# An S4 mixer with a spatial-shift MLP on one core: paired PSUM banks, other parameter and spectrum layouts, a power on GpSimd, and a new order

## The chip, the core and the metric

The kernel runs on one core of one Trainium2 chip. The metric is the device time of one execution in microseconds; the time before is the median of three runs, 515.06 us (515.02 to 515.52). The engines are named as in the profile: PE multiplies matrices (PEld loads its weights beside it), DVE is VectorE, ACT is ScalarE, POOL is GpSimd, SP is SyncE, which here only issues DMAs. Each engine works through its own list of instructions in order.

## The reference, cut to what matters

One sequence of L = 2048 tokens with D = 512 channels, N = 128 states per channel, hidden width F = 1376.

```python
xn = layernorm(u)                                    # over the 512 channels
# A: state-space convolution
K  = einsum("dn,dnl,dn->dl", Cc, exp(dt*A * l), dt*Bc).real     # 512 x 2048, complex inside
y  = irfft(rfft(pad(xn.T)) * rfft(pad(K)))[:L].T + xn * Dskip
# B: spatial shift and MLP, on the same xn
h  = gelu(layernorm(xn) @ w1)                        # 512 -> 512
g  = quarters of h shifted by +1, -1, +2, -2 tokens
x1 = xn + g @ w2
x2 = x1 + gelu(layernorm(x1) @ w3) @ w4              # 512 -> 1376 -> 512
out = u + y * silu(x2)
```

## The kernel before

**Tiling.** X holds the whole sequence in SBUF as 16 tiles of 128 tokens by 512 channels, four bytes an element. Token-side steps take two tiles at a time. The Fourier transforms are matrix products in two stages with DRAM in between: `u_stage1` makes the first stage of the spectrum of xn and stores it to `scr_Ud`; the tables of the convolution kernel end in `scr_Kf`; `products` reads both back, does the second stage, multiplies and does the first inverse stage into `scr_Zd`; `inverse` reads that back and does the last stage.

**Stages.** (1) `loads` and `params`: X, w1 and the parameters come in; six 512 x 128 parameter arrays are read with channel r*128+p in partition p (`raw`, tiles rawA and rawC), DVE and ACT compute on them (tiles tm, pn), PE transposes the result, and ACT copies it into `par`. (2) `token_mixing`: `ln_first` (statistics on DVE, `rstd` as a Sqrt on ACT and a reciprocal on DVE), `x_pair` (transposed tokens), `h_pair` (w1, gelu), `u_stage1`, the scales of w3 and w4 and their split into two halves of 16 bits, `hs_pair` (w2 over shifted tiles, added to X), `ln_second`. (3) 16 chunks of 32 channels in `tables`: sines, cosines and exponentials on ACT, about ten wide products on DVE (tile wv), then matmuls wv into pc and kev into pc and pd. (4) `mlp`, eight groups of 256 tokens, each six steps of w3 (pb), gelu, w4 (pa). (5) `products`, 8 steps for each half of the channels: spectrum of K (kin, into pd in the first half, pc in the second), copy to kh, spectrum of xn (uin, into pd), four DVE operations for the complex product (tiles pr, kh), inverse (pr, into pc and pd), copies to z1e. (6) `gate` (silu on ACT), `inverse` (zin; product into X) and `finish` (X + residual, store).

**PSUM.** Eight banks of 512 columns are eight tiles: pa, pb, pc and pd with two each. A bank is read by an instruction of its own: an evacuation of two banks is two instructions.

**Order.** Nothing is scheduled on the chip. The operations are recorded in program order with their dependencies (`Plan.add`; a PSUM bank counts as one cell for each 32 partitions). ORDER is a written-out list of operation numbers: the engines' instructions are issued in that order, so it fixes each engine's list and what stands behind what. The suffix a or v says which of ACT and DVE takes an operation that both could do (`Either`). All instructions show as L312, the line that issues them, so they are told apart by tiles. Before the first data arrive, 40 dummy matmuls (ident into pa, `WARM`) run on PE.

**Lines that the prediction touches.** `rstd` 576, `loads` 601, `params` 626, `sums` 750 (its end copies pc and pd to k1e), `products` 812, `inverse` 875, `ln_first` 986, `u_stage1` 1053, `hs_pair` 1086, `ln_second` 1104, `mlp` 1130.

Of the kernel before, what the change touches and what calls it, by code (L numbers as in the profile page):

```python
# [110 lines left out]
8 31 0 7 88 3 4 78 89 90 91 22 21 103 105 106 104 92 107 108 2 109 6 93 94 95 5 79 110 111 96a 100a 80 81 82 83 14 112  # L111
113v 84 85 86 17 115v 44 16 42 114a 87a 15 41 43 97a 20 101 98 36 45 46 18 37 118a 72 102a 47 99v 116 48 50 9 51 121
10 122 49 52 23 143 117a 123 53 124 125 54 119 24 164 170 166 171 140 168 25 73a 141 167 165 126 169 551 127 55 172
128 59 173 120a 60 56 11 146 174 175 142 129 19 38 151a 176 27 61 177 57 130 178 39 179v 152a 180v 26 182v 183v 33
148a 144 40 181v 184 186a 131 62 229 28 187 145 147a 192 161 204v 185a 231 154 158 290 188a 132 134 288 70 205 553 150
149 230 292 156 227 153 195 197a 196v 200a 286 375 232 225 287 291 289 71a 293 228 226 294 543 233 295 162 234 544 296
133 235 201a 207a 189 208 373 297 298 199 136v 545 34 299 236 237 190 216 198 63 191 137 217a 193 210 374 202 300 138v
218a 211 304v 203 221v 65 194 64 546 238 371 13 222a 66 68 206 256 135 220 239 219 376 212 139 554 213 67 242v 223
240v 224 257a 258a 262a 261a 209 69 74 555 243v 30 75a 214 215 241v 259 260 277 244v 302v 250 251 278a 58 76 279a 253
252 247v 263 157 264 283a 254 268v 282a 379 245 246 317 248 249 372 163 271 548 549 159 160 265a 547 280 269 550 77a  # L120
# [12 lines left out]
503 518 749 670 495 750 751 686 774 775 516a 671a 672 761 418 701 702 673 755a 756 762a 767a 522a 768 769 770a 763 523
703 519a 687 688 517 524 771a 757 758 776 788 764 765 781 690 772 689 773 782 704 705 674a 675a 777a 520 691 789 692
778 783 525a 779 420 707 784a 785 723 795 802 724 803 693a 694 422 725 676a 706 796 677a 695 708 790a 791 729 678 726
727 728 797 709 526 804 730 780 816a 786 710 787 792 798a 799 805a 806 845 817a 818 696a 697a 794 698a 699a 793 820a
711 712 846 809 731 700 824 825 826 732 810 811 853 847 800 801 812a 713 714 715a 880 854 807 808 813 814 831 815 832
855 716 821a 856 857 849 923 717 718a 838 719a 499 848 819 850 851 822 827a 833 852 823 733 734 858 859 735 736 737a
828 829 830 496 1215 839 860 861 834a 488 720a 721a 477 862 901 902 1222 1223 863 1216 1217 491 840a 474 835 903 738
739 722 740a 741a 836 837 864 867 1224 865 1229 742a 743a 744 1218a 841 866 1236a 842 1225a 882 904 1230 1231 843 1244  # L140
868 869 870 1219 871 906 844 1220 1221 907 872a 944 945 905 873 874 910 875a 876a 1251 946 1226 877a 878a 883 881
1237a 1232a 1227 885a 908 1238 884a 947 948 886 1233 1228 949 1239 887 891 925 1252 888 1245 909 889 890 892 1240a
1241a 893 1246 1234 1235 894 1242 895 898a 912 1258 1247a 879 911 950 953 896a 913 899a 1259 500 1253 1243 897a 914
1265 1254a 1255 915a 900 924 916 917 918a 497 492 489 1266 919a 920a 1248 1249 475 987 478 988 921a 926 968 922 1267
# [1143 lines left out]
```

## Time and profile before

| | |
|---|---|
| median of three runs | 515.06 us |
| the profiled execution, its own time | 514.98 us |
| its span, first to last instruction | 513.1 us |
| busy share of the span: PE, PEld, DVE, ACT, POOL | 96%, 62%, 90%, 79%, 0% |
| ACT_TABLE_LOAD (ACT changes its set of functions) | 54, 69.3 us |
| DMA packets | 156433, of which 98321 under 512 B; 90.07 MB |
| HBM traffic over the span | 160 GB/s |

The span leaves out 1.9 us of the profiled execution's time. A group of instructions is shown as what it writes and reads, shapes, count, then busy time, the mean length of one in ns, and the engine's idle time just before. Lengths overlap where instructions are pipelined: busy time divided by the count is the pitch, and is the better price of one. In tables by stretch the columns are, for each engine, busy us and (instructions), then the granted PE clock, the DMA engines' busy share and GB/s.

### The profile page before, as it was taken

The page shows a single profiled execution, that of the slowest core. Times are in us where ns is not written, and L with a number is a line of the kernel's source. Part 1 is how long each engine was busy: PE and PEld are TensorE (multiplying, and loading weights), DVE is VectorE, ACT ScalarE, POOL GpSimd, SP SyncE. Part 2 cuts the span into 40 slices and gives each one's busy share as a digit, 9 for nine tenths or more (in the row PEclk, how much of TensorE's full clock was granted, in tenths as well). Part 3 has the DMA queues.
Part 4 walks back from the last instruction along what each step waited for, and adds up shares of the span by engine and source line. Part 5 has one row for each costly group of instructions (what it writes and reads, how often), then busy time and mean ns, then how long its engine had stood idle before and what let it go on. Part 6 is the DMA issues. An engine that isn't in the chain of part 4 may idle for free.

```text
span 513.1 us, 14564 instructions
## 1 busy us (share of the span) xinstructions
PE 491.4 (96%) x6209; PEld 315.6 (62%) x6209; DVE 461.7 (90%) x744; ACT 403.4 (79%) x675; POOL 0.7 (0%) x6
## 2 busy tenths in 40 slices
PE   8789999999999999999999999999999999999993
PEld 8656674674446776676566566755665656666541
DVE  4999999999999999999999999999976698777376
ACT  3999999979989899999979999997763652555240
POOL 0000000000000000000000000000000000000000
PEclk9899999999999999999999999999999999999998
DMA  8969997764628613715375556366499997987997
GB/s 215 248 168 260 284 253 242 167 144 125 165 50 170 108 37 42 105 29 76 105 151 119 147 126 123 105 125 187 98 218 220 276 319 213 302 264 223 300 314 201
DMA packets 156433, 90.07 MB, mean 176 GB/s; under 512 B 98321, under 2 KB 147729, under 8 KB 155985
## 3 DMA queue, kind: packets, MB, share of 16 engines
q1 hardware_dynamic: 151840, 84.68, 66.6%
q10 hardware_dynamic: 4528, 4.46, 3.1%
q8 instruction: 49, 0.80, 0.6%
q14 instruction: 16, 0.12, 0.1%
HBM read 52.95 MB, written 29.36 MB: 160 GB/s over the span
## 4 chain that ended last, share of the span: by engine, by line
PE 54%; DVE 35%; ACT 5%; issue 3%; DMA 1%; SPq 0%; DVEq 0%; ACTq 0%
PE pb L312 23%; PE pa L312 16%; DVE wv L312 13%; PE pc L312 10%; PE pd L312 5%; DVE X L312 5%; DVE stats L312 2%; DVE pr L312 2%; DVE ghl L312 2%; DVE eg L312 1%; ACT L312 1%; DVE tm L312 1%; ACT wv L312 1%; DVE kh L312 1%; DMA X<-in_A_u_dram 1%
## 5 line engine op out<-in xcount | busy, mean ns | idle before, releaser
L312 PE MATMUL pb<-x1T,w3h 128*128 128x256 f16 (+1 forms) x1056 | 124.2, 273 | 1.4 <-issue 1.1
L312 PE MATMUL pa<-w4h,ghl 128*128 128x512 f16 (+1 forms) x528 | 122.6, 380 | 0.0
L312 PEld LDWEIGHTS <-w3h 128*128 128x128 f16 (+1 forms) x1056 | 102.0, 100 | 27.3 <-issue 13.1
L312 PEld LDWEIGHTS <-ghl 128*128 128x128 f16 (+1 forms) x528 | 48.9, 98 | 61.5 <-issue 9.0
L312 ACT ACT_TABLE_LOAD x54 | 69.3, 1283 | 3.5 <-issue 2.0
L312 ACT ACTIVATE wv<-wv 128x2080 f32<-128x2080 int32 x32 | 62.8, 1967 | 1.6 <-DVE wv L312 1.5
L312 DVE SCALAR_TENSOR_TENSOR ghl<-g,wsc,ghl 128x512 f16<-128x512 f32 (+1 forms) x48 | 33.3, 698 | 6.6 <-ACT ghl L312 6.5
L312 ACT ACTIVATE g<-pb,wsc 128x512 f32<-128x512 f32 (+1 forms) x48 | 30.5, 652 | 9.7 <-PE pb L312 5.4
L312 DVE TENSOR_TENSOR wv<-wv,eg 128x2048 f32<-128x2048 f32 x16 | 36.5, 2284 | 1.2 <-ACT wv L312 1.1
L312 DVE TENSOR_TENSOR wv<-mag,wv 128x2048 f32<-128x2048 f32 x16 | 36.5, 2283 | 0.0
L312 ACT ACTIVATE ghl<-g,wsc 128x512 f16<-128x512 f32 (+1 forms) x37 | 26.1, 707 | 10.7 <-PE pa L312 8.0
L312 PEld LDWEIGHTS pc<-wv 128*32 128x32 f32 x2048 | 29.8, 109 | 6.6 <-issue 2.4
L312 ACT ACTIVATE mag<-par 128x128 f32<-128x128 f32 x132 | 32.8, 459 | 0.9 <-DVE wv L312 0.9
L312 PE MATMUL pc<-wv 128*32 128x64 f32 x2048 | 32.4, 220 | 0.7 <-DVE wv L312 0.6
L312 ACT ACTIVATE wv<-wv,halfpi 128x2080 f32<-128x2080 f32 x16 | 32.9, 2056 | 0.2
L312 PE MATMUL pb<-xT,w1h 128*128 128x256 f16 x240 | 27.7, 273 | 0.0
L312 DVE TENSOR_TENSOR pr<-pd,kh 128x512 f32<-128x512 f32 x32 | 20.6, 685 | 7.6 <-PE pd L312 7.2
L312 PE MATMUL pa<-w,hT 128*128 128x512 f32 x58 | 26.3, 597 | 0.8 <-ACT ue L312 0.8
L312 PEld LDWEIGHTS <-w1h 128*128 128x128 f16 x240 | 22.8, 98 | 6.0 <-issue 2.6
L312 PE MATMUL pb<-w,hT 128*128 128x512 f32 x58 | 26.4, 596 | 0.0
L312 DVE BATCH_NORM_STATS2 stats<-X 128x6 f32<-128x512 f32 x32 | 21.3, 679 | 5.5 <-DMA X<-in_A_u_dram 5.5
L312 ACT COPY z1e<-pc 128x256 f32<-128x256 f32 x24 | 8.7, 381 | 21.6 <-PE pd L312 21.6
(158 smaller groups left out, 848.1 us busy)
## 6 DMA issues: line engine op xcount, KB each, us to landing
wst<-in_B_w_dram SPq DMA_DIRECT2D x20, 512.0 KB, 4.8
scr_Ud<-ue SPq DMA_DIRECT2D x32, 256.0 KB, 3.0
uin<-scr_Ud SPq DMA_DIRECT2D x16, 512.0 KB, 4.8
scr_Kfa<-k1e SPq DMA_DIRECT2D x8, 512.0 KB, 5.0
cst<-c_gp SPq DMA_DIRECT2D x16, 256.0 KB, 5.2
kin<-scr_Kfa SPq DMA_DIRECT2D x8, 512.0 KB, 4.4
scr_Kfb<-k1e SPq DMA_DIRECT2D x8, 512.0 KB, 6.6
scr_Zda<-z1e SPq DMA_DIRECT2D x8, 512.0 KB, 3.6
```

What stands on the lines that cost most here:

```text
L312: ins = [getattr(self.engines[op.eng], name)(*args, **kw).ins for name, args, kw in op.calls]
```

## The change

- **Paired banks.** Each pair of PSUM banks is also one tensor of 1024 columns (`two`). Where both banks of a pair were read one after the other, one instruction reads both: the copies ue, kh, k1e and z1e, the complex product, the additions in `hs_pair` and `mlp`, the product in `inverse`.
- **Parameters.** Partition p now holds channels 4p to 4p+3, so each row of an array is 2 KB in one piece where it was four pieces of 512 B; log_dt comes as 128 pieces of four numbers where it was 512 single ones. The copy into `par` puts the channels back in order.
- **Spectra.** `scr_Ud` keeps all 512 channels of a token together: one store for each tile (16 of 512 KB) where there were two (32 of 256 KB). The reads take half of each row.
- **Reciprocal roots.** In `ln_first` from tile 4 on and in `ln_second`, Sqrt on ACT and reciprocal on DVE become two instructions on POOL: add EPS, then raise to -0.5.
- **Order.** ORDER is new throughout.

By engine the program has: PE the same matmuls; DVE 746 instructions, now 630; ACT 682, now 588, with 54 and 47 ACT_TABLE_LOAD; SP 226, now 210; POOL 11, now 23.

DVE at the start. rawC holds B and C, tm products of them, stats the norm's statistics, X the tokens. Before:

```order
L312 BN_STATS stats<-X 128x6
L312 MEMSET epst 128x1
L312 MEMSET ones 1x128
L312 MEMSET ssq 128x16
L312 BN_AGGR mv<-stats 128x2
L312 TENSOR_SCALAR rs<-mv 128x1
L312 RECIPROCAL rs<-rs 128x1
```

And now:

```order
L311 TENSOR_TENSOR tm<-rawC 128x512 x3
L311 TENSOR_TENSOR tm<-tm 128x512
L311 TENSOR_TENSOR tm<-rawC 128x512
L311 BN_STATS stats<-X 128x6
L311 BN_AGGR mv<-stats 128x2
L311 TENSOR_SCALAR rs<-mv 128x1
L311 RECIPROCAL rs<-rs 128x1
```

Five products on the parameters, which stood behind the first four tiles' statistics, now stand ahead of the first. On SP, whose list began with four loads of X, the four of rawC now come first (two halves of X still go out on ACT's queue at once):

```order
L311 DMA rawC<-in_A_C_re_dram 128x512
L311 DMA rawC<-in_A_B_re_dram 128x512
L311 DMA rawC<-in_A_C_im_dram 128x512
L311 DMA rawC<-in_A_B_im_dram 128x512
L311 DMA X<-in_A_u_dram 64x512 x2
L311 DMA X<-in_A_u_dram 64x1024 x2
```

ACT in the first norm, tiles 8 to 15 (rs is the reciprocal root, ue the evacuated first stage, hT the gelu). Before:

```order
L312 ACTIVATE x2h<-X,rs 128x512
L312 ACT_TABLE_LOAD
L312 ACTIVATE rs<-mv,epst 128x8 x2
L312 ACT_TABLE_LOAD
L312 ACTIVATE hT<-pb_94 128x512
L312 COPY ue<-pa_91 128x512
L312 ACTIVATE wst,ssq<-wst 128x1024
L312 COPY ue<-pa_92 128x512
```

And now, about the same place:

```order
L311 ACTIVATE hT<-pb 128x512
L311 ACTIVATE wst,ssq<-wst 128x1024
L311 COPY ue<-pd 128x1024
L311 COPY ue<-pa 128x1024
L311 ACT_TABLE_LOAD
L311 ACTIVATE mag<-par 128x128 x11
```

The two roots and the pair of table loads around them are gone, and a copy takes two banks.

DVE at the end, from the last addition of the MLP (X<-pa) on. Before, its first rows:

```order
L312 SCALAR_TENSOR_TENSOR X<-pa_91,wsc,X 128x512
L312 SCALAR_TENSOR_TENSOR X<-pa_92,wsc,X 128x512
L312 TENSOR_TENSOR X<-X,pd_98 128x256
L312 TENSOR_TENSOR X<-X,pd_97 128x256
L312 TENSOR_TENSOR X<-X,pc_96 128x256
L312 TENSOR_TENSOR X<-X,pc_95 128x256
L312 TENSOR_TENSOR X<-X,pd_97 128x256
L312 TENSOR_TENSOR X<-X,xr 128x4x256
```

And now:

```order
L311 SCALAR_TENSOR_TENSOR X<-pa,wsc,X 128x1024
L311 TENSOR_TENSOR X<-X,pd 128x2x256
L311 TENSOR_TENSOR X<-X,pc 128x2x256
L311 TENSOR_TENSOR X<-X,pd 128x2x256
L311 TENSOR_TENSOR X<-X,xr 128x4x256
```

Behind the last addition there are ten `inverse` products and six `finish` additions in both orders; the products were 20 instructions and are 10.

The diff, without ORDER's rows and the bookkeeping of banks:

```diff
-    bank = [[ps.tile([P, D], F32, name=f"p{n}{i}") for i in range(2)] for n in "abcd"]
+    two, bank = [], []
+            t = places.enter_context(nc.psum_tensor(f"p{n}", [P, 2, D], F32))
+            two.append(t[:])
...
+    def power(dst, var):
+        G.tensor_scalar(var, var, EPS, None, op0=ALU.add)
+        e = half if len(dst.shape) == 2 else half.unsqueeze(2)
+        G.tensor_tensor(dst, var, e.to_broadcast(list(dst.shape)), op=ALU.pow)
...
-            Q.dma_start(raw[n], src.rearrange("(r p) n -> p r n", p=P))
-        Q.dma_start(ld, log_dt.rearrange("(r p) -> p r", p=P))
+            Q.dma_start(raw[n].rearrange("p r n -> p (r n)"), src.rearrange("(p r) n -> p (r n)", p=P))
+        Q.dma_start(ld, log_dt.rearrange("(p r) -> p r", p=P))
...
-            E.copy(par[:, k], pt)
+            E.copy(par[:, k].rearrange("n (p r) -> n r p", r=4), pt.rearrange("n (r p) -> n r p", r=4))
...
-        for r in range(4):
-            E.copy(k1e[:, :, 8 * r : 8 * r + 8], pk[r][:, :DH].rearrange("p (i d) -> p i d", d=8))
+        for k in range(2):
+            E.copy(
+                k1e[:, :, 16 * k : 16 * k + 16].rearrange("p i (r d) -> p r i d", r=2),
+                two[2 + k][:, :, :DH].rearrange("p r (i d) -> p r i d", d=8),
+            )
...
-            for t, dr in ((uin, Ud[hf]), (kin, K1d[hf])):
+            for t, dr in ((uin, Ud[..., hf * DH : hf * DH + DH]), (kin, K1d[hf])):
...
-            kh = [ring["kh"]([P, 2, DH], F32, "kh") for _ in range(2)]
-            for h in range(2):
-                E.copy(kh[h], kp[h])
+            kh = ring["kh"]([P, 2, 2, DH], F32, "kh")
+            E.copy(kh, kp)
...
-                V.tensor_mul(t, up[h], kh[h])
-                V.tensor_mul(kh[h][:, ::-1], up[h], kh[h][:, ::-1])
-                V.tensor_sub(t[:, 0], t[:, 0], t[:, 1])
-                V.tensor_add(t[:, 1], kh[h][:, 0], kh[h][:, 1])
+            V.tensor_mul(z, up, kh)
+            V.tensor_mul(kh[:, :, ::-1], up, kh[:, :, ::-1])
+            V.tensor_sub(z[:, :, 0], z[:, :, 0], z[:, :, 1])
+            V.tensor_add(z[:, :, 1], kh[:, :, 0], kh[:, :, 1])
...
-            for c in range(4):
-                E.copy(z1e[:, c], pz[c])
+            for k in range(2):
+                E.copy(z1e[:, 2 * k : 2 * k + 2], two[2 + k][:, :, :DH])
...
-        for a in range(2):
-            Xh = X[:, 2 * g + a, ch]
-            V.tensor_mul(Xh, Xh, py[a])
+        Xh = X[:, 2 * g : 2 * g + 2, ch]
+        V.tensor_mul(Xh, Xh, two[k][:, :, :DH])
...
-        rstd(r12[:, ss], mv[:, ss, 1:3])
+        if ss.start < 4:
+            rstd(r12[:, ss], mv[:, ss, 1:3])
+        else:
+            power(r12[:, ss], mv[:, ss, 1:3])
...
-            for r in range(2):
-                E.copy(ev_t[:, r], pu[2 * a + r])
-            for h in range(2):
-                Q.dma_start(
-                    Ud[h, :, :, s + a], ev_t[:, :, h * DH : (h + 1) * DH]
-                )
+            E.copy(ev_t, two[3 * a])
+            Q.dma_start(Ud[:, :, s + a], ev_t)
...
+        V.tensor_add(X[:, s0 : s0 + 2], X[:, s0 : s0 + 2], two[k % 2])
...
-            V.tensor_add(X[:, s], X[:, s], acc[i])
...
-        rstd(r3[:, ss], mv[:, ss, 1])
+        power(r3[:, ss], mv[:, ss, 1])
...
-        for i in range(2):
-            s = 2 * g + i
-            V.scalar_tensor_tensor(X[:, s], accs[i], a4, X[:, s], op0=ALU.mult, op1=ALU.add)
+        V.scalar_tensor_tensor(X[:, 2 * g : 2 * g + 2], two[0], a4, X[:, 2 * g : 2 * g + 2], op0=ALU.mult, op1=ALU.add)
...
+    V.memset(half, -0.5)
```

More of the change, by code (lines that the diff above doesn't have):

```diff
@@ L116 @@
[L116 to L120, printed above, removed]
@@ L185, in __init__ @@
     def __init__(self, nc):
-        self.engines = {"PE": nc.tensor, "ACT": nc.scalar, "DVE": nc.vector, "SP": nc.sync}
+        self.engines = {
+            "PE": nc.tensor, "ACT": nc.scalar, "DVE": nc.vector, "SP": nc.sync, "POOL": nc.gpsimd,
+        }
         self.ops = []
         self.cells = {}
+        self.banks = {}
         self.stage = None
@@ L214, in cover @@
         if "PSUM" in space:
-            return {(t.name, "bank", q) for q in quarters}
+            a, z = self.banks[t.name]
+            if z - a == 1:
+                return {(a, "bank", q) for q in quarters}
+            up = sum(step * (n - 1) for step, n in dims[1:] if step > 0)
+            lo, hi = first // D, (first + up) // D
+            return {(a + k, "bank", q) for k in range(lo, hi + 1) for q in quarters}
         base = t.manual_sbuf_range[0]
@@ L423 @@
     plan = Plan(nc)
-    V, A, T, Q = [Engine(plan, e) for e in ("DVE", "ACT", "PE", "SP")]
+    V, A, T, Q, G = [Engine(plan, e) for e in ("DVE", "ACT", "PE", "SP", "POOL")]
     E = Either(plan)
@@ L483 @@
     ssq = keep([P, 16], "ssq")
+    half = wsc[:, 15:16]
     Dt = keep([P, NCH, 8], "Dt")
@@ L554 @@
     assert o + 12 * K4 <= END
-    bank = [[ps.tile([P, D], F32, name=f"p{n}{i}") for i in range(2)] for n in "abcd"]
+    two, bank = [], []
+    with ExitStack() as places:
+        for k, n in enumerate("abcd"):
+            t = places.enter_context(nc.psum_tensor(f"p{n}", [P, 2, D], F32))
+            two.append(t[:])
+            plan.banks[t.name] = 2 * k, 2 * k + 2
+    for k, n in enumerate("abcd"):
+        bank.append([])
+        for i in range(2):
+            t = nc.alloc_psum_tensor(f"p{n}{i}", [P, D], F32)
+            bank[k].append(t[:])
+            plan.banks[t.name] = 2 * k + i, 2 * k + i + 1
     turn = {"mm": 0, "kg": 0, "pp": 0, "t": 0, "sc": 0}
@@ L777, in sums @@
         due(f"ks{cc}")
-        pk = bank[2] + bank[3]
+        pk = [two[2 + r // 2][:, r % 2] for r in range(4)]
         k1e = k1er([P, NI, CQ], F32, "k1e")
@@ L878, in inverse @@
         Q.dma_start(zin, Zd[hf][:, 2 * g : 2 * g + 2].rearrange("p s r d -> p (s r) d"))
-        py = [t[:, :DH] for t in pp_pair()]
+        turn["pp"] += 1
+        k = 2 + turn["pp"] % 2
+        py = [two[k][:, a, :DH] for a in range(2)]
         with plan.together(cost=0.55):
@@ L1053, in u_stage1 @@
     def u_stage1(s):
-        pu = bank[0] + bank[3]
+        pu = [two[3 * (r // 2)][:, r % 2] for r in range(4)]
         with plan.together(cost=QUAD):
@@ L1086, in hs_pair @@
     def hs_pair(s0, k):
-        acc = bank[k % 2]
+        acc = [two[k % 2][:, i] for i in range(2)]
         for i in range(2):
@@ L1132, in mlp @@
         x1T = x1Ts.pop(i_g)
-        accs = bank[0]
+        accs = [two[0][:, i] for i in range(2)]
         for jp in range(6):
```

150 lines of the change are left out of this document (71 added, 79 removed), and 3 rows, old and new, of the table ORDER.

## The prediction

> **What bounds the kernel now.** I read the page's first lines, then the table by stretch, then the groups of PE.
>
> ```profile
> span 513.1 us, 14564 instructions
> PE 491.4 (96%) x6209; PEld 315.6 (62%) x6209; DVE 461.7 (90%) x744; ACT 403.4 (79%) x675; POOL 0.7 (0%) x6
> 0.00:13.20 13.20, 11.85 (x80) 11.85 (x81) 6.48 (x31) 4.69 (x8) 0.70 (x6) 1.00 0.90 219
> 13.20:19.40 6.20, 3.02 (x18) 2.55 (x17) 6.08 (x10) 5.97 (x11) 0.00 (x0) 0.85 1.06 272
> 19.40:50.00 30.60, 28.12 (x130) 19.92 (x131) 30.50 (x92) 30.39 (x64) 0.00 (x0) 0.97 0.87 214
> 50.00:100.00 50.00, 47.88 (x383) 29.54 (x380) 48.69 (x69) 49.62 (x85) 0.00 (x0) 1.00 0.97 249
> 100.00:240.00 140.00, 139.98 (x1671) 89.88 (x1672) 138.97 (x186) 131.01 (x222) 0.00 (x0) 1.00 0.46 93
> 240.00:360.00 120.00, 118.52 (x1950) 75.50 (x1949) 119.09 (x152) 112.01 (x183) 0.00 (x0) 1.00 0.57 132
> 360.00:480.00 120.00, 118.11 (x1833) 74.16 (x1831) 90.09 (x171) 62.55 (x100) 0.00 (x0) 1.00 0.86 239
> 480.00:494.00 14.00, 14.00 (x80) 7.03 (x80) 7.79 (x15) 4.64 (x6) 0.00 (x0) 1.00 1.04 295
> 494.00:513.10 19.10, 9.88 (x81) 5.12 (x80) 14.05 (x28) 2.54 (x3) 0.00 (x0) 0.89 0.83 248
> ```
>
> PE is busy almost without a break from 19.4 to 494. Its idle time there is the difference in each row: 2.5 us to 50, 2.1 to 100, none to 240, 1.5 to 360, 1.9 to 480, in sum 8.0. A busy PE can still be a waiting one, so I compare the pitch of its largest group with its best stretch (from the chain of waits, start and length):
>
> ```profile
> L312 PE MATMUL pb<-x1T,w3h 128*128 128x256 f16 (+1 forms) x1056 | 124.2, 273 | 1.4 <-issue 1.1
> 60.98 2.62 PE pb L312 x24
> ```
>
> 124.2/1056 is 0.118 us, and 2.62/24 is 0.109 for the same width: little hides in the busy time, and part of that little is the switch from one kind of matmul to the next, of which both orders have 242. The change alters no matmul. So the time is PE's work plus three things that it can move: the start up to 19.4, the 8.0 us of waits, and the tail of 19.1. DVE is as full as PE from 13 to 360 (30.50 of 30.60, 138.97 of 140), ACT to 100; behind 360 both have room. Savings on them count only where PE waits for them.
>
> **What the merged instructions and the power take off.** The prices are pitches, busy time by count, from the groups:
>
> ```profile
> L312 ACT ACT_TABLE_LOAD x54 | 69.3, 1283 | 3.5 <-issue 2.0 <-ACT X L312 0.6
> L312 ACT COPY z1e<-pc 128x256 f32<-128x256 f32 x24 | 8.7, 381 | 21.6 <-PE pd L312 21.6
> L312 ACT COPY kh<-pd 128x512 f32<-128x512 f32 x16 | 8.6, 590 | 2.6 <-PE pd L312 2.6
> L312 ACT ACTIVATE X<-X 128x1024 f32<-128x1024 f32 x8 | 8.2, 1053 | 4.5 <-DVE X L312 4.5
> L312 DVE TENSOR_TENSOR pr<-pd,kh 128x512 f32<-128x512 f32 x32 | 20.6, 685 | 7.6 <-PE pd L312 7.2
> L312 DVE TENSOR_TENSOR pr<-kh 128x256 f32<-128x256 f32 x32 | 13.2, 424 | 0.9
> L312 DVE TENSOR_TENSOR up<-mag 128x1024 f32<-128x1024 f32 x16 | 19.5, 1217 | 0.1
> L312 DVE TENSOR_SCALAR X<-X,rs,bs 128x512 f32<-128x512 f32 x13 | 6.7, 539 | 0.0
> L312 ACT ACTIVATE X<-X,bs,rs 128x512 f32<-128x512 f32 x3 | 2.3, 805 | 0.0
> L312 DVE RECIPROCAL rs<-rs x15: 155/171/196, 5.2 to 415.0; 128x2 f32<-128x2 f32 x4, 128x4 f32<-128x4 f32 x4, 128x8 f32<-128x8 f32 x4, 128x1 f32<-128x1 f32 x2
> L312 ACT ACTIVATE rs<-mv,epst x9: 279/298/306, 9.5 to 412.2; 128x8 f32<-128x8 f32 x4, 128x2 f32<-128x2 f32 x3, 128x4 f32<-128x4 f32 x1, 128x6 f32<-128x6 f32 x1
> masks.py:199 POOL TENSOR_SCALAR_AFFINE_SELECT ident<-ident 128x128 f32<-128x128 f32 x1 | 0.3, 292 | 0.1
> ```
>
> On ACT two copies of 256 cost 0.73 and one of 512 costs 0.54; two of 512 cost 1.08 and one of 1024, by the silu's row, 1.03. So a merge is worth 0.05 to 0.19. About 77 merges at 0.14 are 11 us; seven table loads at 1.28 are 9.0; six roots at 0.30 are 1.8. On DVE a pair of 512 costs 1.29 against 1.22 (0.07), a pair of 256 costs 0.83 against 0.64 (0.18): 32 merges of the first kind and 32 of the second in the complex products are 8 us; the additions in the MLP and the products of the last stage add some 4. Each engine loses 3 to 5% of its work, little of it where PE waits. No row shows a power on POOL. The nearest is the select of 128 elements in 0.29 us, for 8 elements less; above I allow 2 us for each of the six pairs. Root, table loads and reciprocal that it replaces took 0.3 + 2 x 1.28 + 0.2, so between a gain of 2.7 and a loss of 1 in the latency of one norm; with tokens loaded ahead I take nothing.
>
> The Trainium skill's page "ScalarE: Activation LUTs", section "What ACT_TABLE_LOAD costs", puts a drain of about 1.38 us beside the load's 1.28, so 2.66 for a switch. This trace agrees on the load and shows no drain: the idle time before all 54 is 3.5 us, 0.06 each. By the page the seven loads would give ACT 18.6 us and not 9.0, and with two of them in the first stage (below) the sum would be 509.8 where I get 512.6; on rows alone that lies with rival (1).
>
> **From 0 to 100.** This is where the order changes most, and both signs are possible.
>
> ```profile
> 4.08 0.69 DVE L312 BATCH_NORM_STATS2 stats<-X 128x6 f32<-128x512 f32 x1 [3.08 <-DMA X<-in_A_u_dram]
> 1.35 12.02 PE L312 MATMUL pa<-ident 128*128 128x128 f32 x80 [1.35 <-POOL ident masks.py:199]
> 9.48 0.30 ACT L312 ACTIVATE rs<-mv,epst 128x2 f32<-128x2 f32 x1 [6.21 <-DVE mv L312]
> 12.92 1.89 DVE L312 TENSOR_TENSOR tm<-rawC 128x512 f32<-128x512 f32 x3
> 17.64 1.11 PE L312 MATMUL pc<-ident,pn 128*128 128x128 f32 x4 [2.65 <-DVE pn L312]
> 19.41 2.66 PE L312 MATMUL pb<-xT,w 128*128 128x256 f32 x8
> 22.45 3.62 PE L312 MATMUL pb<-xT,w 128*128 128x256 f32 x16
> 15.00:18.00 3.00, 0.35 (x2) 0.36 (x3) 2.93 (x5) 2.85 (x6) 0.00 (x0) 0.92 1.02 229
> 18.00:21.00 3.00, 3.00 (x12) 2.72 (x11) 2.95 (x7) 2.97 (x7) 0.00 (x0) 0.51 1.00 219
> ```
>
> Now rawC's megabyte goes first. With 0.25 MB of X beside it, at the 219 GB/s of the first row, it is there 5.7 us after the first packets at 2.3 (estimate: 8.0; by bigger pieces perhaps 6). Five products at 0.63 (1.89/3) then run ahead of the first statistics, the first two or three before the last array lands: the statistics start near 10, not 4.08. Their followers, 1.4 us of them up to the root, bring ACT's first root to about 12, not 9.48; the first real matmul of w1 (19.41) moves by about as much, 2 to 2.5 us. What waits behind the statistics on DVE is X's normalisation, then ACT's copy, then PE's transposes and w1. That is the loss.
>
> Against it, DVE works in 5 to 9 us where it sat idle for X, 1.5 us more by 13.2, and in 19.4 to 100 both feeders have less to do. ACT loses two table loads (2.6), three roots (0.9) and 1.5 in 14 pairs of ue, and takes three normalisations from DVE (three fewer there, three more here, 0.8 each): 2.6 net. DVE loses those three at 0.5, three reciprocals, and is ahead by 1.5. Since DVE and ACT are 99% busy from 19.4 to 100 while PE has 4.6 us of idle, the end of this stretch is theirs: ACT ends it 2.6 earlier less the 1.5 that it starts later (2.5, of which it fills 1 with the two absolute values that moved ahead), so **-1.0 us**. Bounds: -4.6, PE's idle, and +3.8, below. The copies into `par` write with steps of four elements; no row shows whether that is slower, and four of them at 0.6 would cost 2.4 more on ACT if it doubled, which the upper bound holds.
>
> ```profile
> 31.89 0.60 SPq L312 DMA_DIRECT2D scr_Ud<-ue  x1
> PEld L312 <- DMA scr_Ud<-ue: 0.8, 1, 0.8
> ```
>
> Stores of spectra: 16 issues fewer on SP at 0.6 us, larger pieces. The one wait of PE's that ends at such a store is 0.8 us, so nothing.
>
> **From 100 to 480.** In 100 to 360 DVE loses about 4 us in the products of the first half and 2 in the additions; PE waits 1.5 there. I take **-0.8**, between 0 and -1.5. In 360 to 480 DVE is at 75%, and PE's 1.9 are links between kin, kh, uin, pr and z1e. One copy of 1.03 is done when the second of two was (1.08), and the next spectrum writes both banks in turn, so it needed both before too; **-0.3**, between -1.9 and +1.9. The MLP's joined addition holds pa for 1.3 us where the first bank was free after 0.7, but in the new order 24 or more matmuls of w3 (2.6 us), once 12 of them and a chunk's 128 of wv, stand ahead of the next group's use of pa.
>
> **The tail.** From the last addition on DVE alone sets the pace:
>
> ```profile
> 493.73 1.40 DVE L312 SCALAR_TENSOR_TENSOR X<-pa,wsc,X 128x512 f32<-128x512 f32 x2
> 495.06 0.75 DVE L312 TENSOR_TENSOR X<-X,pd 128x256 f32<-128x256 f32 x2
> 507.97 0.69 DVE L312 TENSOR_TENSOR X<-X,xr 128x512 f32<-128x512 f32 x1
> ```
>
> A pair of products took 0.75, one of twice the width 0.68 (512 wide, as the last row): ten times 0.07. The joined addition saves 0.1 but starts 0.3 later, when both banks are summed, and the third product follows the first on pd with only one between, 0.7 us for an answer of PE of over 1.0. **-0.3**, between -0.8 and +0.8.
>
> **Sum.** -1.0 - 0.8 - 0.3 - 0.3 = -2.4 on the profiled execution's 514.98 (span 513.1 and 1.9 around it): 512.6 us. The median before is 515.06, so the same scale.
>
> **Rivals.** (1) All waits go: a new order with lighter feeders closes PE's 8.0 us of idle and the tail's 0.8: 506.2. For it, DVE and ACT are the waits' likely cause to 360; against it, 1.9 lie where both have room and each cure moves the next wait in. (2) Nothing arrives: PE has all the work that it had, the late start eats what the feeders save, 514 to 516. For it, the 139.98 of 140. (3) The start decides, slower. PE's first matmul of w1 comes 2.1 later or more, and the pause after the dummy matmuls (13.4) lengthens. The row 15 to 18 shows PE nearly idle and the next a clock of 0.51, in which eight matmuls took 2.66 where sixteen took 3.62 later: a slow stretch of 3.4 us costs 1.7. One more such stretch and the 2.1 give +3.8, and with ACT's gain lost too, 514.98 + 3.8 = 518.8. It decides if the first w1 matmul starts after 22.4, three later than now, which is more than ACT's 2.6 can make good. (4) The change doesn't do what it says: the power on POOL takes far longer than 2 us and holds up the norms; three of them at 5 would be 515 to 518, in (2) and (3).
>
> The Trainium skill's page "TensorE: Matmul & The Clock Gate", section "The HAM clock gate (the "warmup" mystery)", has the clock halved after an idle window of about 3.4 us; the 0.51 agrees. It speaks for (3), since the new order leaves PE with less to do up to 20.
>
> **Chances.** 0.42 for the sum's case (511 to 514.0), 0.20 for (1) and what lies towards it, 0.20 for (2), 0.18 for (3). Runs of this kernel spread by 0.5 us, so 0.2% (1.0 us) is about what can be told from none: faster 0.62, within 0.2% 0.20, slower 0.18. The range runs from 507.5, a large part of (1), to 517.0, half of (3)'s way. The likeliest case's own range is 511 to 514.
>
> **What would show it.** Right: ACT near 387 us busy, 47 table loads, DVE near 448, PE's busy time as before; PE's idle in 19.4 to 100 under 3.6, in 100 to 360 under 1; the first w1 matmul at 21 to 22; the last addition to the end 19 us. Wrong: a first w1 matmul after 22.4 or a second slow stretch of the clock; a POOL row of several us with DVE's normalisation behind it; new waits of PE for z1e, kh or k1e; or a stretch from 19.4 to 494 that is shorter by more than 4, which would say that more of PE's busy time was waiting than I read.

## The result and the profile after

The changed kernel takes 523.07 us (median of four runs, 520.37 to 524.34) where the kernel before took 515.20 beside it: a ratio of 1.0145, with a 95% interval of 1.0124 to 1.0166. Forecast were 512.6 and a range up to 517.0. The change is slower by 7.9 us.

The first lines of its page, profiled at 523.77 us:

```profile
span 522.0 us, 14337 instructions
PE 493.9 (95%) x6209; PEld 316.7 (61%) x6209; DVE 452.9 (87%) x628; ACT 390.8 (75%) x581; POOL 19.4 (4%) x18
```

The feeders did lose their work: DVE 8.8 us of 461.7, ACT 12.6 of 403.4. The span grew by 8.9 all the same. The table by stretch of the same run, columns as before:

```profile
13.20:19.40 6.20, 1.84 (x11) 1.01 (x9) 5.99 (x24) 6.02 (x12) 0.00 (x0) 0.87 1.04 246
19.40:50.00 30.60, 26.74 (x114) 18.79 (x115) 23.56 (x69) 30.45 (x59) 4.84 (x4) 0.86 0.76 202
50.00:100.00 50.00, 45.95 (x376) 30.06 (x375) 48.54 (x70) 45.69 (x71) 2.69 (x2) 1.00 0.78 230
100.00:240.00 140.00, 135.77 (x1612) 85.00 (x1611) 134.87 (x183) 122.07 (x201) 5.08 (x2) 1.00 0.51 103
240.00:360.00 120.00, 119.87 (x1924) 78.41 (x1923) 118.21 (x126) 111.65 (x155) 4.60 (x2) 1.00 0.56 118
360.00:480.00 120.00, 118.55 (x1881) 73.37 (x1880) 92.57 (x115) 61.77 (x75) 1.55 (x2) 1.00 0.86 234
494.00:522.00 28.00, 19.33 (x130) 10.03 (x128) 16.84 (x22) 4.04 (x5) 0.00 (x0) 0.96 0.77 218
```

PE's idle time is the length of a stretch less its busy time:

| stretch, us | before | after | difference |
|---|---|---|---|
| 13.2 to 19.4 | 3.18 | 4.36 | +1.2 |
| 19.4 to 50 | 2.48 | 3.86 | +1.4 |
| 50 to 100 | 2.12 | 4.05 | +1.9 |
| 100 to 240 | 0.02 | 4.23 | +4.2 |
| 240 to 480 | 3.37 | 1.58 | -1.8 |
| from 494 | 9.22 | 8.67 | -0.5 |

That is 6.4 us more of idle time. The other 2.5 are PE's busy time, 493.9 where it was 491.4: the same matmuls at a mean granted clock of 0.988 where it was 0.993. So the loss lies ahead of 240, and what is behind it gives two back. The numbers between 19.4 and 50 already speak against the prediction's picture of that stretch: DVE was busy for 23.56 of 30.60 us, not 30.50. Of the two feeders ACT was as full as before (30.45, where it was 30.39); DVE stood.

The start, from the timeline after:

```profile
21.88 3.22 PE L311 MATMUL pb<-xT,w 128*128 128x256 f32 x8
```

The first statistics at 10.44 (forecast "near 10"), the first root at 12.42 ("about 12"), the first w1 matmul at 21.88 ("21 to 22"): as worked out. What was not worked out is how long the granted clock stays at half. Two rows of the change:

```profile
22.00:30.00 8.00, 8.00 (x35) 6.53 (x35) 7.97 (x23) 7.95 (x20) 0.36 (x1) 0.84 0.99 212
44.00:47.00 3.00, 2.96 (x9) 0.99 (x10) 0.00 (x0) 2.99 (x9) 1.13 (x1) 0.67 0.93 321
```

Before, the clock is 1.00 in both stretches: the half clock of the start ended at 21 us. In the change it lasts to about 24.6 (an estimate from the first row: a mean of 0.84 over 8 us is 2.6 us at half), and it comes a second time behind 45. The rest of the damage is behind the start. From the timeline, 39 to 57 us:

```profile
39.04 1.11 ACT L311 COPY par<-pc 128x512 f32<-128x512 f32 x1
39.22 1.13 PE L311 MATMUL pa<-X,ks 64*128 64x512 f32 x4
40.18 1.02 PE L311 MATMUL pd<-X,ks 64*128 64x512 f32 x4
41.00 1.08 ACT L311 ACTIVATE wst<-wst 128x1024 f32<-128x1024 f32 x1
42.04 1.03 ACT L311 COPY ue<-pd 128x1024 f32<-128x1024 f32 x1
42.93 1.05 ACT L311 COPY ue<-pa 128x1024 f32<-128x1024 f32 x1
44.04 1.13 PE L311 MATMUL pa<-X,ks 64*128 64x512 f32 x4 [2.83 <-ACT ue L311]
46.80 4.52 PE L311 MATMUL pb<-xT,w 128*128 128x256 f32 x16
51.36 1.26 DVE L311 TENSOR_TENSOR wv<-par,ev 128x1056 int32<-128x1056 f32 x1 [7.66 <-PE pb L311]
53.17 3.72 PE L311 MATMUL pb<-xT,w 128*128 128x256 f32 x16
```

PE writes the first-stage block of one pair of tiles to pa and pd (39.22, 40.18), and the next thing in its list is the next such block. That needs pa again, and pa is free when the joined copy at 42.93 has ended, which stands on ACT behind another copy, a weight square and two more. PE idles for 2.83 us. Behind the pause sixteen matmuls take 4.52 us that take 3.72 at 53.17: 0.8 us lost at the lower clock. And DVE stands for 7.66 us, because wv lies where w1 lay and waits for those sixteen to read it. In the order before the sixteen stood between two blocks, and PE did not pause:

```profile
37.84 3.72 PE L312 MATMUL pb<-xT,w 128*128 128x256 f32 x16
41.49 1.13 PE L312 MATMUL pa<-X,ks 64*128 64x512 f32 x4
```

The Trainium skill's page "TensorE: Matmul & The Clock Gate", section "The HAM clock gate (the "warmup" mystery)", puts the clock at half after an idle window of about 3.4 us. This trace agrees only in part: the pause here is 2.83 us, shorter than that, and the half clock starts behind it, while PE is working again. Nor does the pause always bring it. In the run with w3h moved (below) the same pause stands at the same place, and the sixteen run at full clock:

```profile
43.59 1.13 PE L311 MATMUL pa<-X,ks 64*128 64x512 f32 x4 [2.83 <-ACT ue L311]
45.51 3.72 PE L311 MATMUL pb<-xT,w 128*128 128x256 f32 x16
```

The second place, from the timeline 112 to 123 us:

```profile
114.81 4.10 PE L311 MATMUL pb<-xT,w1h 128*128 128x256 f16 x36
119.74 1.16 ACT L311 ACTIVATE w3h<-wst,wsc 128x1024 f16<-128x1024 f32 x1
120.95 1.49 PE L311 MATMUL pb<-xT,w1h 128*128 128x256 f16 x12 [2.03 <-ACT w3h L311]
```

The last twelve matmuls of w1 wait 2.03 us for ACT's conversion of a w3 tile, from which they take nothing. Before, all 48 of that group ran in one piece:

```profile
107.34 5.41 PE L312 MATMUL pb<-xT,w1h 128*128 128x256 f16 x48
```

The instructions that the prediction had no row for, or priced, from the groups after:

```profile
L311 POOL TENSOR_TENSOR rs<-mv,wsc 128x8 f32<-128x8 f32 (+2 forms) x6 | 12.1, 2014 | 0.5
L311 POOL TENSOR_SCALAR mv<-mv 128x8 f32<-128x8 f32 (+2 forms) x6 | 6.7, 1112 | 411.2 <-DVE mv L311 400.5 <-DVE bs L311 10.6
L311 ACT ACT_TABLE_LOAD x47 | 60.3, 1283 | 3.0 <-issue 2.2
L311 ACT COPY par<-pc 128x512 f32<-128x512 f32 x4 | 4.3, 1085 | 0.0
```

A joined copy into kh takes 1.01 us and a joined product into pr 1.22, as priced. The copy into par takes 1.085 us with steps of four elements, where it took 0.62.

### The profile page after: what moved, and what is told of

Read it like the earlier page. It is cut to its first block, busy times and chain, and to the rows that moved or that the text cites. A ratio compares the mean times of both kernels' runs of the same rounds, so it can differ in the third digit from the quotient of the medians.

```text
span 522.0 us, 14337 instructions
## 1 busy us (share of the span) xinstructions
PE 493.9 (95%) x6209; PEld 316.7 (61%) x6209; DVE 452.9 (87%) x628; ACT 390.8 (75%) x581; POOL 19.4 (4%) x18
## 4 chain that ended last, share of the span: by engine, by line
PE 66%; DVE 18%; issue 3%; ACT 3%; DMA 2%; POOL 1%; DVEq 0%; POOLq 0%
PE pb L311 25%; PE pa L311 23%; PE pc L311 12%; DVE wv L311 7%; PE pd L311 6%; DVE X L311 4%; DVE x2h L311 1%; DMA uin<-scr_Ud 1%; DMA scr_Zda<-z1e 1%; DVE eg L311 1%; DVE up L311 1%; DVE w1h L311 1%; ACT ue L311 1%; DVE pab L311 1%; POOL mv L311 1%
## 5 line engine op out<-in xcount | busy, mean ns | idle before, releaser
L311 ACT ACTIVATE ghl<-g,wsc 128x512 f16<-128x512 f32 (+1 forms) x35 | 23.9, 685 | 12.1 <-PE pa L311 7.7
L311 DVE TENSOR_TENSOR pr<-pd,kh 128x1024 f32<-128x1024 f32 x16 | 19.6, 1223 | 13.5 <-ACT kh L311 10.5
L311 DVE TENSOR_TENSOR wv<-par,ev 128x1056 int32<-128x1056 f32 x16 | 20.0, 1253 | 7.7 <-PE pb L311 7.7
L311 PE MATMUL pb<-xT,w 128*128 128x256 f32 x96 | 24.7, 411 | 0.2 <-ACT hT L311 0.2
```

The lines of the kernel that those rows point to most:

```text
L311: ins = [getattr(self.engines[op.eng], name)(*args, **kw).ins for name, args, kw in op.calls]
```

## The experiments

### Parts and order, each without the other

Two theories at first. ORDER: the new order loses the time, whatever the parts. PARTS: joined copies that must wait for both banks, strided copies and powers lose it, whatever the order. Two transplants tell them apart.

**The parts in the old order.** The change's program with its numbers in the sequence of before (first row shown):

```diff
 ORDER = """
-2 0 4 5 16 3 15 42 18 45 17 43 8 44 46 9 89 90 91 7 92 47 93 94 48 95 6 80 81 49 96 97a 82 83 84 85 51 86 79 87 23 22
+4 9 32 0 8 89 3 5 79 90 91 92 23 22 104 106 107 105 93 108 109 2 110 7 94 95 96 6 80 111 112 97a 101a 81 82 83 84 15
...
```

> All four parts of the change stay (joined banks, parameters by four, one store per spectrum, the power on GpSimd), but the work goes out in the order of the kernel before: a joined instruction stands where the later of its two halves stood. Theory ORDER (the 7.6 us that PE loses up to 160 us come from the new order: the second first-stage block of the spectra directly behind the first, statistics behind the six products): the loss goes, 511 to 515 us, and what the parts are worth shows, 0 to -4. Theory PARTS (a joined copy must wait for both banks and stands behind other work on ScalarE, the copies with steps of four, the powers): the loss stays, 519 to 523. Theory POWER (only the powers): the loss stays for the most part, 518 to 521.

Measured: 530.31 us, ratio 1.0309 (1.028 to 1.0337).

**The order with the old parts.** The kernel before with its numbers in the sequence of the change:

```diff
 ORDER = """
-8 31 0 7 88 3 4 78 89 90 91 22 21 103 105 106 104 92 107 108 2 109 6 93 94 95 5 79 110 111 96a 100a 80 81 82 83 14 112
+2 0 4 15 3 14 41 17 44 16 42 7 43 45 8 88 89 90 6 91 46 92 93 47 94 5 79 80 48 95 96a 81 82 83 84 50 85 78 86 22 21
...
```

> The opposite: the kernel before, its instructions unjoined and its roots on ScalarE and VectorE, sent out in the order of the change; the halves of a joined instruction follow each other. ORDER: 521 to 526 us, the loss is all here and the unjoined work adds up to 3 to it. PARTS: 513 to 517. POWER: 513 to 516.

Measured: 529.19 us, ratio 1.0287 (1.0264 to 1.031). Each theory is refuted by the other's run: the parts alone cost 15.4 us, the order alone 14.3, both together 7.9. What a part is worth depends, then, on the order that it stands in. So the parts were priced in both.

### The power on GpSimd

**Undone in the change** (two instructions for two, at the same places):

```diff
-        if ss.start < 4:
-            rstd(r12[:, ss], mv[:, ss, 1:3])
-        else:
-            power(r12[:, ss], mv[:, ss, 1:3])
+        rstd(r12[:, ss], mv[:, ss, 1:3])
...
-        power(r3[:, ss], mv[:, ss, 1])
+        rstd(r3[:, ss], mv[:, ss, 1])
```

> The change with the six powers on GpSimd put back to a root on ScalarE and a reciprocal on VectorE, two instructions for two, at the same places of the order. POWER: 516 to 519 us, and the waits of 9 to 13 us behind the second norm at 145 to 160 are gone. ORDER and PARTS: 521 to 524, since PE lost only 1.1 us beside the slowest power; the seven table loads come back on ScalarE.

Measured: 527.52 us, ratio 1.0245 (1.0221 to 1.027), 4.5 above the change. The power is a gain here. ACT has the seven loads again (54 of 1.283 us), 9.0 us, and the time grew by half of that; that the loads are the way was not tried apart. The Trainium skill's page "ScalarE: Activation LUTs", section "What ACT_TABLE_LOAD costs", would make the seven 18.6 us with its drain; in the change's group above ACT is idle for 3.0 us ahead of all 47, so no drain shows.

**Alone in the kernel before**, the reverse of that diff in the old order:

> The kernel before with the power on GpSimd alone, six pairs for six, in the old order; all other instructions as before. If what the tables cost ScalarE decides (it loses 7 loads and 6 roots, 10.8 us of work): 511 to 514. If the latency of the power decides (2.4 to 5.1 us for a pair in the change's trace, against some 0.5 us and a load before), in an order made for the short root: 517 to 522.

Measured: 519.06 us, ratio 1.0082 (1.0053 to 1.011), so 3.8 lost. From the timeline of this run:

```profile
28.45 0.95 POOL L312 TENSOR_SCALAR mv<-mv 128x8 f32<-128x8 f32 x1 [27.17 <-DVE wsc L312]
29.49 1.67 POOL L312 TENSOR_TENSOR rs<-mv,wsc 128x8 f32<-128x8 f32 x1
31.19 0.17 DVE L312 TENSOR_SCALAR rs<-rs 128x2 f32<-128x2 f32 x1 [1.83 <-POOL rs L312]
34.33 1.66 PE L312 MATMUL pd<-ident,x 128*128 128x128 f32 x8 [3.03 <-DVE x L312]
```

And the same place before:

```profile
28.68 0.30 ACT L312 ACTIVATE rs<-mv,epst 128x8 f32<-128x8 f32 x1
29.23 0.19 DVE L312 RECIPROCAL rs<-rs 128x8 f32<-128x8 f32 x1
32.77 1.06 PE L312 MATMUL pd<-ident,x 128*128 128x128 f32 x8 [1.19 <-DVE x L312]
```

From variance to root took 0.7 us (28.68 to 29.42) and takes 2.7 (28.45 to 31.16). DVE waits for it, and so does PE, 1.8 us longer. The same part costs 3.8 us in the old order and gains 4.5 in the new one. In the old order the rows show its latency at work; that ACT's time decides in the new one is argued from the loads.

### The parameters

**Undone in the change:**

```diff
-            Q.dma_start(raw[n].rearrange("p r n -> p (r n)"), src.rearrange("(p r) n -> p (r n)", p=P))
+            Q.dma_start(raw[n], src.rearrange("(r p) n -> p r n", p=P))
...
-            E.copy(par[:, k].rearrange("n (p r) -> n r p", r=4), pt.rearrange("n (r p) -> n r p", r=4))
+            E.copy(par[:, k], pt)
```

> The change with the parameters loaded as before (channel r*128+p at partition p) and copied into par without the step of four; same order. PARTS with the strided copies as the cause: four copies at 0.62 instead of 1.10 us on ScalarE at 36 to 59 us, where PE waits 2.8 us for the copies of ue behind them: 519 to 521 us. ORDER: 521 to 524, and the small pieces of the loads may even delay the first statistics, by up to 1.

Measured: 520.14 us, ratio 1.0124 (1.0081 to 1.0168), 2.9 under the change, but the interval is wide and reaches into that of the change, so the gain is not clear of the spread. A copy into par takes 0.587 us here.

**Alone in the kernel before**, the reverse:

> The kernel before with the parameters four channels per partition alone, in the old order: bigger pieces in the loads, and four copies into par with steps of four (1.10 us in the change's trace, not 0.62). If the copies' 1.9 us on ScalarE before 60 us come through: 516 to 517.5. If they lie in waits: 514.5 to 515.5. If the earlier loads decide: 512 to 514.

Measured: 516.69 us, ratio 1.0029 (1.0017 to 1.0041): 1.5 lost. Four copies at 0.5 us more are 2.0; the bigger pieces of the loads do not make them good.

### The joined banks

**Alone in the old order** (the first transplant with the power and the parameters undone by the two diffs above; the joined stores of the spectra are still in it):

> The joined banks and the joined stores of the spectra alone, in the order of the kernel before: roots on ScalarE and VectorE and parameters as before. If the three parts add up in the old order (15.4 us all together, 3.8 for the power, 1.5 for the parameters): 524 to 526. If a joined instruction costs nothing where its later half stood (what the prediction said of them: every second half is done when it was): 513 to 516, and the sum comes from parts that meet. ORDER and PARTS as before: 513 to 515 and 520 to 526.

Measured: 529.18 us, ratio 1.0267 (1.025 to 1.0284). The three parts are not a sum here: 13.9 + 3.8 + 1.5 would be 19.2, and together they are 15.4. But the banks, with the joined stores, are nearly all of it. The prediction's sentence that the second half is done when it was holds for the end of a copy and not for the next use of the banks. Two places of the timeline:

```profile
85.31 8.80 PE L311 MATMUL pa<-w,hT 128*128 128x512 f32 x16 [2.61 <-DMA w<-in_B_w_dram]
128.33 1.21 DVE L311 TENSOR_TENSOR X<-X,pb 128x1024 f32<-128x1024 f32 x1
129.60 3.70 PE L311 MATMUL pb<-w,hT 128*128 128x512 f32 x8 [1.32 <-DVE wsc L311]
```

At 128 us the joined addition starts when PE has summed both banks, and then PE waits, 1.32 us, until it has read both (the row names wsc, an instruction of DVE that ends beside the addition). With two instructions DVE reads one bank while PE fills the other. Before, PE goes on without a pause around the addition at 120.24:

```profile
112.59 10.47 PE L312 MATMUL pb<-w,hT 128*128 128x512 f32 x24
120.24 0.68 DVE L312 TENSOR_TENSOR X<-X,pb 128x512 f32<-128x512 f32 x1
```

At 85 us PE waits for a load of w2. On SP's list it stands behind a store of a spectrum, now a joined one, and it goes out at 79.80 where it went at 76.63. Its table by stretch:

```profile
100.00:240.00 140.00, 135.43 (x1605) 85.07 (x1604) 131.96 (x176) 124.06 (x200) 0.00 (x0) 1.00 0.45 91
240.00:360.00 120.00, 115.48 (x1768) 75.08 (x1774) 114.56 (x125) 111.39 (x156) 0.00 (x0) 1.00 0.54 116
```

PE idles for 4.57 us in the first stretch, where it had 0.02, and for 4.52 in the second, where it had 1.48. In the whole span it idles for 33.0 us, where it did for 21.7. The two places are a part of that; copies of z1e, for which PE waits 3.5 us where it waited 0.5, are another. How much the joined reads cost and how much the joined stores was not tried apart.

**Undone in the new order** (the kernel before with power and parameters as in the change, and the change's sequence; the stores of the spectra are separate again too):

```diff
-            E.copy(kh, kp)
+            for h in range(2):
+                E.copy(kh[h], kp[h])
...
```

> The change's order with its power and its parameters, but separate banks: every joined instruction is two again, one directly behind the other. If the joining is worth in this order what the unchanged halves cost more (0.05 to 0.19 us for each of some 150): 525 to 530, since the same order with all parts old took 529.2 and undoing the power alone took 4.5 of that. If the joined waits are what costs: 517 to 521.

Measured: 525.79 us, ratio 1.0216 (1.0183 to 1.0248). Joining is worth 2.7 us in the new order. So the new order carries the parts: two of the three are a gain in it. What loses is then to be looked for in the order itself, at single places.

### The places of the order

Theory QUEUE: single places make PE wait and can be moved. Rival FEEDERS: ACT and DVE set the end of the first 100 us, and a wait that is taken away comes back later.

**w1 between the blocks.** 209 is the third first-stage block, 186 and 187 the sixteen matmuls of w1, 514 the exponentials on ACT:

```diff
-... 272 223 209 65 224 514 186 187 270 ...
+... 272 223 186 187 209 65 224 514 270 ...
```

> The change with one move: TensorE's two groups of w1 (16 matmuls into pb that need nothing new of ScalarE) stand ahead of the third first-stage block of the spectra and no longer behind it. Theory QUEUE (the loss at 39 to 52 us is the place: block behind block, so TensorE waits 2.8 us for the two joined copies that stand behind 3.4 us of other work on ScalarE, then runs at the half clock, and VectorE waits 7.7 us for those w1 groups): TensorE's wait there falls under 0.5, VectorE's under 2, and the time to 517 to 520 us. Theory FEEDERS (ScalarE and VectorE set the pace to 100 us whatever TensorE's order): the wait only turns up later, 521.5 to 524.

Measured: 519.49 us, ratio 1.0104 (1.0044 to 1.0164), 3.6 under the change. Its timeline:

```profile
41.11 3.72 PE L311 MATMUL pb<-xT,w 128*128 128x256 f32 x16
44.86 1.26 DVE L311 TENSOR_TENSOR wv<-par,ev 128x1056 int32<-128x1056 f32 x1 [1.21 <-PE pb L311]
49.86 2.08 PE L311 MATMUL pa<-X,ks 64*128 64x512 f32 x4 [3.12 <-ACT ue L311]
```

The sixteen run at full clock, DVE goes on 6.5 us earlier. The next two blocks in a row now wait in their turn, 3.12, so PE's own pause has only moved. What went is idle time behind it: in 50 to 100 us PE idles for 0.27 us, where it did for 4.05. The single runs lie from 517.18 to 523.84 (the change's from 520.37 to 524.34), so the 3.6 alone is not clear of their spread.

**w3h behind the last readers.** 420 is the conversion on ACT, 324 the last twelve matmuls of w1. No engine's own list changes by this:

```diff
-... 551a 420a 324 421 325 ...
+... 551a 324 420a 421 325 ...
```

> The change with one number of the table moved by one place: the conversion w3h on ScalarE is listed behind the last twelve matmuls of w1, not ahead. The order on every engine stays; only TensorE's wait for w3h (2.0 us at 121 us; w3h lies where the first weights w1h lay, whose last readers these matmuls are) goes. If TensorE's waits before 160 us add up to the loss: 520.5 to 521.5 us. If the next wait takes it over: 522.5 to 523.5.

Measured: 520.28 us, ratio 1.0099 (1.007 to 1.0127), 2.8 under the change. From its timeline:

```profile
112.74 5.41 PE L311 MATMUL pb<-xT,w1h 128*128 128x256 f16 x48
```

All 48 matmuls run in one piece, which ends at 118.15, beside the conversion that starts at 117.66. PE's idle time in 100 to 240 falls from 4.23 to 2.35. w3h lies where w1h lay, and the matmuls listed behind it read other columns of that place, so they need not wait. But a wait is made for each tile that shares a place with one written earlier in the list. The plan's own dependencies, which are by pieces of 128 bytes, hold no such edge; the program's semaphores do. Compared with these dependencies, PE has no such wait in the program before and two in the change. The other makes later matmuls of w1 wait for wv, whose first instruction on DVE itself stood 7.66 us.

**Both, and then the parameters as before with them** (the two diffs above together, then with that of the parameters):

> The change with the first two of these alone, so that all its parts stay and two places of its order are other. Adding up: 516 to 518. One slack: 519 to 520.5.

Measured: 516.51 us, ratio 1.0039 (1.0025 to 1.0053). 6.6 under the change, far outside the spread of both, where the two alone gave 3.6 and 2.8: they add up.

> The change with three things at once that each brought 2.8 to 3.6 us alone: w1 matmuls ahead of the third first-stage block, w3h listed behind the last readers of its place, parameters as before. If they add up: 513.5 to 515.5 us, the kernel before. If they are one slack seen three times (ScalarE and VectorE end the first 100 us, as the run with the early order by hand says): 518 to 520.

Measured: 516.13 us, ratio 1.002 (1.0 to 1.0039); single executions spread from 512.28 to 517.6. The parameters bring 0.4 here, not 2.9, and neither is clear of the spread. Those copies stood on ACT ahead of the one that PE waited for, so the likely reading is that they and the first place were one wait. Rows of the run with the two places, profiled at 515.55:

```profile
19.40:50.00 30.60, 27.13 (x124) 18.99 (x125) 28.66 (x84) 30.45 (x62) 6.68 (x6) 0.94 0.74 209
50.00:100.00 50.00, 48.45 (x381) 31.41 (x378) 48.35 (x61) 49.55 (x75) 0.85 (x1) 1.00 0.85 237
100.00:240.00 140.00, 137.45 (x1651) 87.91 (x1649) 135.95 (x182) 123.20 (x197) 5.08 (x2) 1.00 0.49 98
```

PE's idle time is 1.55 in 50 to 100 (4.05 in the change, 2.12 before) and 2.55 in 100 to 240 (4.23, 0.02), and the clock in the first row is 0.94 where it was 0.86. PE is busy for 490.8 us in all, where it was for 493.9 in the change.

**The early stretch by hand.** As the three, with all blocks of 38 to 55 us parted by w1 matmuls, pa copied ahead of pd, and the exponentials on ACT behind the copies (the main moves):

```diff
-... 209 65 224 514 186 187 270 ... 196 212a 157 194 210a 245 517 ... 515 516 ...
+... 186 187 188 209 65 224 270 ... 194 196 210a 212a 157 517 206 207 203 204 208 245 205 514 ...
```

> The change with old parameters, w3h behind the last matmuls of w1, and between 39 and 55 us a new order by hand: the first-stage blocks of the spectra 2 and 3 each have w1 matmuls in front of them, pa is copied ahead of pd, and the exponentials on ScalarE stand behind the copies. QUEUE: TensorE's waits from 38 to 60 us fall from 6.4 to under 2 and the half clock goes: 513 to 516.5. FEEDERS: 518 to 520.

Measured: 523.39 us, ratio 1.0146 (1.0125 to 1.0166): all given back. From its timeline:

```profile
59.48 2.08 PE L311 MATMUL pa<-X,ks 64*128 64x512 f32 x4 [3.07 <-ACT ue L311]
```

And its table by stretch:

```profile
46.00:52.00 6.00, 6.00 (x28) 4.67 (x25) 6.00 (x19) 2.62 (x3) 2.60 (x2) 1.00 1.03 338
```

PE no longer waits from 46 to 52 us, as expected, but now ACT waits for PE: it is busy for 2.62 of these 6 us, and 2.86 more go by at 53.94. Its exponentials come late, the copies of ue and the transposed x2h behind them too, and PE pays 3.07 at 59 and 3.35 at 66 us.

**Blocks apart, ACT's list kept.** As the three, with 206 and 207 between the third block and the fourth (245):

```diff
-... 210a 245 517 344 ... 211 206 207 35 ...
+... 210a 517 206 207 245 344 ... 211 35 ...
```

> As the three undone, and two more matmul groups of w1 between the second and the third block, so that no two first-stage blocks follow each other up to 52 us; ScalarE's order stays. QUEUE: 2 to 3 us under the three undone. FEEDERS: the same as these within 1.

Measured: 518.23 us, ratio 1.0062 (1.0044 to 1.0081), 2.1 worse than the three. FEEDERS is right for this stretch once the first place is mended: PE can be served earlier only at the cost of something behind.

**pa ahead of pd** on ACT for the second and the third block:

```diff
-... 343 195a 32 33 193a 273 ... 196 212a 157 194 210a 245 ...
+... 343 193a 195a 32 33 273 ... 194 196 210a 212a 157 245 ...
```

> As the three undone, and ScalarE copies pa ahead of pd for the second and third block (with the stores in the same order), since TensorE's next block writes pa first. QUEUE: the wait of 3.1 us for the copy at 50 us loses about 1 and the half clock behind it may go: 514 to 515.5. FEEDERS (the copies end when they did): 515.5 to 516.5.

Measured: 516.15 us, ratio 1.0025 (1.0008 to 1.0042): no difference from the three.

### The start

**The old start in the change**, and with the early stretch by hand (the first hundred steps as before, then the change's sequence):

```diff
-2 0 4 5 16 3 15 42 18 45 17 43 8 44 46 9 89 90 91 7 92 47 93 94 48 95 6 80 81 49 96 97a 82 83 84 85 51 86 79 87 23 22
+4 9 32 0 8 89 3 5 79 90 91 92 23 22 104 106 107 105 93 108 109 2 110 7 94 95 96 6 80 111 112 97a 101a 81 82 83 84 15
...
```

> The change with the first hundred steps sent out as before (X's first megabyte and its statistics ahead of the six products of the parameters), everything behind in the change's order. First real matmul of w1 near 19.5 and not 21.9. Theory START (what TensorE loses up to 22 us is lost for good): 520 to 521.5. Rival (the waits for ue at 39 to 44 us take it back, since ScalarE is full up to there): 522.5 to 524.

Measured: 522.05 us, ratio 1.0134 (1.0108 to 1.0159). The first w1 matmul came at 20.00 us, 1.9 earlier, and 1.0 of it is left at the end. The long half clock of the start is still there (a mean clock of 0.51 from 17 to 24 us), so it does not come from the new start alone.

> As the run before it, and the first hundred steps as before the change. START and QUEUE together: 511 to 514, under the kernel before. If the start is taken back by ScalarE: the same as the run before it.

Measured: 522.21 us, ratio 1.0131 (1.0115 to 1.0147), 1.2 under that stretch without it.

> As the run before it, and the first hundred steps as before the change. The old start brought 1.0 us alone, less than the 2.3 by which its first w1 matmul came earlier. If it adds up: 513 to 514.5, under the kernel before. If ScalarE takes it back: the same as the run before it within 0.7.

Measured: 515.00 us, ratio 1.0002 (0.9988 to 1.0016), 1.15 under the same without the old start. Three times about 1 us, each within a run's spread. With the two places, the parameters and the start put back, the change is the kernel before: joined banks, joined stores, powers and a new order together bring nothing that can be measured. No version here beats it.

## Why the prediction was wrong

**The start (right in time, small in effect).** Statistics, root and first w1 matmul came when worked out. The old start is worth 1.0 to 1.2 us, within the bounds. Rival (3) named the right sign, and one of its two signs showed: a second stretch of half clock, at 45 us, beside a longer one at the start. But its condition, a first w1 matmul after 22.4, did not come (21.88), and its price, +3.8, is half of the loss. The loss had another place.

**From 0 to 100, -1.0 us: the step that failed.** Its argument was "since DVE and ACT are 99% busy from 19.4 to 100 ..., the end of this stretch is theirs". It took ACT's work off the end. In the change DVE had 7 us of idle time up to 50 and ACT, full to 50, had 4.3 from 50 to 100. What set the time was who stands behind whom: two first-stage blocks in a row on PE, and ahead of the copies that they need a par copy, a weight square and two other instructions on ACT, and behind them the sixteen matmuls for which DVE's wv waits. So DVE, full before, stands for 7.66 us because PE is late, and PE is late because of what ACT does first. The order of the change was there to be read; the prediction looked at the norm's rows at this place and not at PE's. Undoing that one place brought 3.6 us. The bound, +3.8, was made from the start alone and left this term out.

**The par copies.** The upper bound held 2.4 us "if it doubled". It went from 0.62 to 1.085, 1.9 us for four, and cost 1.5 in the old order. In the change it is likely a part of the wait for ue: 2.9 alone, 0.4 once that wait is mended. It should have been in the sum and not only in the bound.

**From 100 to 480, -0.8 and -0.3.** Behind 240 it was right: PE's idle time fell by 1.8 against 1.1 forecast for 100 to 480. Ahead of it the prediction could see no loss, since PE had 0.02 us of idle time there: it went to 4.23. Half is the wait for w3h, which no engine's list shows, because it comes from the place in the common list. That cost 2.8. The cause of the other half stays open: with both places mended PE still idles for 2.55 us there.

**The banks: "it needed both before too".** True for the spectrum's copies, and the step stopped there. In the old order the joining, with its stores, costs 13.9 us, so it is not harmless in itself; the new order is what makes it worth 2.7.

**The power: "take nothing".** The bounds were a gain of 2.7 and a loss of 1 for one norm, at 2 us a pair. The six pairs took 3.1 us each (12.1 + 6.7 over six), one of them 5.1. In the old order the norms were held up, as rival (4) had it, and that cost 3.8. Yet it is not what lost here: in the change the power gains 4.5, more than the whole forecast gain of 2.4.

**The tail, -0.3.** From the joined addition to the end there are 18.5 us, where there were 19.4: 0.9 less, a little past its bound.

```profile
503.49 1.28 DVE L311 SCALAR_TENSOR_TENSOR X<-pa,wsc,X 128x1024 f32<-128x1024 f32 x1 [4.11 <-PE pa L311]
```

**Rival (2), nothing arrives,** is what the mended order shows: 515.00.

The sum: of the 7.9 us the two places took 6.6 (3.6 and 2.8 alone) and the start about 1. The 2.5 us of PE's busy time are not a term beside them: with the two places mended it is 490.8 us, no more than before. What brings the half clock in one run and not in another stays open, since the same pause of 2.83 us was followed by it in the change and not in the run with w3h moved.

## What to carry to other kernels

When an order is replaced along with the instructions, price each part in both orders: here the same three parts cost 15 us in one and brought gains of 4.5 and 2.7 in the other. Don't argue from how busy the feeders are; walk PE's new list, and for each group ask which instruction frees its bank and what stands ahead of that instruction on its engine. A joined read of two banks can take away the overlap between the engine that fills and the one that empties, as at 128 us above, so look for other work for PE to be listed between two uses of the pair.

## What was not expected

- A list's place can make a wait where no engine's own order changes: one number moved by one place took 2.8 us off.
- ACT writes 128x512 from PSUM with steps of four elements in 1.085 us, in one piece in 0.587 to 0.623.
- The power on GpSimd took 1.2 to 3.4 us for 2 to 8 elements a partition, and not by their number; the addition ahead of it took 0.4 to 3.4:

```profile
145.24 3.41 POOL L311 TENSOR_SCALAR mv<-mv 128x8 f32<-128x8 f32 x1 [86.72 <-DVE mv L311]
258.93 3.43 POOL L311 TENSOR_TENSOR rs<-mv,wsc 128x6 f32<-128x6 f32 x1
```

What makes the long ones long was not tried.
